# Sparse attention with routed experts: a reordered addition, a step timetable for the side jobs, and routing moved between engines

## The chip, the core and the metric

The kernel runs on one core of a Trainium2 chip. The core has four compute engines that work side by side, each through its own queue in order: TensorE (PE, with its weight loads as PEld), VectorE (DVE), ScalarE (ACT) and GpSimd (POOL). SyncE (SP) issues most of the DMAs. The metric is the device time of one execution in microseconds (us); lower is better.

## The reference

```python
scores = scale * np.matmul(q, k.transpose(0, 1, 3, 2))      # 8 batches, 8 heads, 576 x 576, d = 64
kth = np.partition(scores, -top_k, axis=-1)[..., -top_k:-top_k + 1]   # top_k = 32
scores = np.where(scores >= kth, scores, -1000000000.0)
attn = np.exp(scores - np.max(scores, axis=-1, keepdims=True))
attn = attn / (np.sum(attn, axis=-1, keepdims=True) + 1e-09)
x = np.matmul(attn, v)                # heads joined: 4608 tokens of 512
logits = x @ w_gate                   # 8 experts
expert_idx = np.argmax(logits, axis=1)
# gate_w = softmax(logits) at expert_idx
out[mask] = gate_w[mask, None] * (np.maximum(x[mask] @ w1[e], 0.0) @ w2[e])   # for each expert e
```

Attention keeps the 32 largest scores of each row. Each token then goes to the one expert with the largest logit.

## The kernel before

**Attention** runs as one loop of 144 steps. A step handles two tiles of 128 query rows with 576 scores each; nine steps make a quarter (four heads of a batch), 36 steps a pair of batches. The loop is software-pipelined: in iteration t, PE makes the scores of step t+3 (`ps`), which ACT copies to `sb`; DVE searches step t (24 `MAX8` of 48 columns a step into `vq`, line 1079, then a merge, lines 450, 1082 and 1086, whose last three reductions are carried into the next iteration as `delayed`); POOL makes the thresholds `nb` from the merge; ACT writes a sign mask `sg` for each of the two tiles of step t-2 with the threshold as bias, and counts the kept scores (line 494); POOL adds the mask to the scores (line 495), which sends the small ones far down; PE transposes step t-3 (`tt`, line 501), ACT takes the exponential (`et`, line 505), and PE multiplies by V (`px`, line 515).

**Side jobs** are Python generators in lanes. `advance` is called once a step; it goes through the lanes in the order of their due times (`DUE`), takes one stage of each lane whose needs (shared PSUM banks, spots, and planner's units of us per engine) fit under `LIMITS`, and queues its instructions. `at=` restricts a stage to given steps of the nine. The names ahead of a profile row show the jobs, all recorded by the helper in line 280:

- `prep`: turns Q and K for the next scores (`rq`, `rk`, `lqk` to `qk`).
- `sums` and `rows`: the softmax sums, then the finished rows turned back, scaled (`xm`, `lp`, `xl`, `lpl`) and stored to DRAM as tokens `xs` and partial logits `lps`.
- `find`: for each pair of batches, rows whose count of kept scores isn't 32 are flagged (`r_key`, `r_ok`, `r_qx`) and fetched (`r_sb`).
- `redo`: four rounds of `MAX8` and `MATCH_REPLACE8` over the 576 scores of up to 128 flagged rows, then their exponential.
- `patch`: turns the flagged rows (`r_et`), multiplies them by V (40 matmuls in one run), turns the result (`r_xa`) and overwrites their rows of `xs` and `lps`.
- `route`: loads the pair's logits (`ll`), finds each token's expert (`lg`, `sh`, `oh`), counts tokens per expert with a history of one-hots (`hist`, `cum`), ranks them on PE, and scatters each token's entry to `table` in ten indirect DMAs (line 899).

Lanes take the pairs one after another. PSUM has two shared banks for jobs, one bank for the scores' left parts, and three banks `tt`, of which the last 384 columns (SMALL) are a spot for small results. Such work is queued as `pe_late`, behind the step's transposes.

**The expert stage (MoE)** works in units: an expert and a number of 128-token tiles. Each unit runs eight chunks of the hidden size; a chunk loads 512 KB of weights, splits them into high and low parts (ACT line 1009, DVE 1011 and 1012, POOL 1012), and runs `hidden` (line 1264) and `project` (line 1279) with three products each. `EARLY` names units that start on part of the batches: an entry (5, 1, 2) is one expert, two tiles, from the first four batches (8 - 5 + 1); (3, 4, 3) is four experts, three tiles, from the first six. Full units have five tiles, and the rest of an early expert's tiles follows later. At the attention's end the jobs left over are drained stage by stage, one round of lanes between two chunks of the early units. When all are routed, `over` makes a table of overflow tiles.

Of the kernel before, what the change touches and what calls it, by code (L numbers as in the profile page):

```python
# [23 lines left out]
TOPK = 32  # L24
# [3 lines left out]
A0, A1, A2, A3 = -4, 1, 2, 2  # L28
EARLY = ((5, 1, 2), (3, 4, 3))
# [26 lines left out]
def attention_moe(ctx, tc, q, k, v, w_gate, w1, w2, out):  # L56
# [117 lines left out]
    nc.gpsimd.iota(eight, pattern=[[1, 8]], base=0, channel_multiplier=0, allow_small_or_imprecise_dtypes=True)  # L174
    stat = consts.tile([128, B, 3], F32, name="stat")
# [101 lines left out]
    cell, small, held, att_open = [1], [1], [0], [True]  # L277
# [13 lines left out]
    def need(**k):  # L291
        return k
# [43 lines left out]
    def j_prep(p):  # L336
# [151 lines left out]
    def softmax(t, us, i):  # L488
# [6 lines left out]
        nc.gpsimd.tensor_tensor(SB[u], SB[u], SG[i], op=OP.add)  # L495
# [45 lines left out]
    def j_sums(n):  # L541
# [17 lines left out]
        yield need(slack=1)  # L559
# [117 lines left out]
    def j_find(p):  # L677
# [31 lines left out]
        vec(nc.vector.tensor_tensor, oh, slots[:, None, 0:64].to_broadcast([128, 16, 64]),  # L709
            sl.rearrange("p j x -> p (j x)")[:, :, None].to_broadcast([128, 16, 64]), op=OP.is_equal)  # L710
# [29 lines left out]
    def turn(x, name, w=512):  # L740
        pt = bank()
        xf = x.rearrange("p h d -> p (h d)")
        for c in range(HP):
            pe(nc.tensor.transpose, pt[:, c * 128:(c + 1) * 128], xf[:, c * 128:(c + 1) * 128], ident)
        xt = jobs.tile([128, w], F32, name=name, bufs=1)[:, 0:512]
        act(nc.scalar.activation, xt, pt, AF.Copy)
        act(release, pt)
        return xt

    def j_redo(p):  # L750
# [28 lines left out]
    def j_patch(p, ex, nb, qi, hmb):  # L779
        sm = lambda name, shape, dt=F32: jobs.tile(shape, dt, name=name, bufs=1)  # L780
        et = sm("r_et", [128, KB * 128]).rearrange("p (c q) -> p c q", c=KB)
        yield need(bank=1, nook=1, pe=0.6, act=0.7, dve=0.2, at=FREE)
        vec(nc.vector.tensor_scalar, nb[:, 1:2], nb[:, 1:2], 1e-9, None, op0=OP.add)
        vec(nc.vector.reciprocal, nb[:, 2:3], nb[:, 1:2])
        pt = bank()
        for c in range(MAIN):
# [25 lines left out]
        yield need(bank=1, pe=0.5, act=0.5, at=FREE)  # L812
        xt = turn(xa, "r_et", KB * 128)
# [28 lines left out]
    def j_route(p):  # L842
# [11 lines left out]
        yield  # L854
        yield need(dve=0.8)
# [6 lines left out]
        cum = small("cum", [128, E, KR + 1], BF)  # L862
        vec(nc.vector.tensor_reduce, lg, ll.rearrange("p i (h e) -> p i e h", h=H), axis=AX.X, op=OP.add)
# [754 lines left out]
```

## Time and profile before

| | |
|---|---|
| median of 3 runs | 1284.72 us (1282.67 to 1284.81) |
| the profiled execution's own time | 1284.31 us, of which the profile's span is 1282.4 |
| busy: PE, DVE, POOL, ACT | 1164.8, 957.6, 843.3, 813.8 us |
| first and last exponential of the 144 steps | 40.0 and about 765 us |

A row of instructions reads: line, engine, operation, output<-inputs, shapes, count | busy time, mean ns of one | idle time of the engine just before them and what ended it. A row of waits reads: who waited, for whom: us in total, times, longest. A row of a timeline is start, length, instruction, and in brackets the idle time before it. Only the engine that ends last in a stage sets its time; idle time of the others is free.

### The profile page before, as it was taken

What the parts mean: (1) busy time and instruction counts of PE and PEld (TensorE: products, weight loads), DVE (VectorE), ACT (ScalarE), POOL (GpSimd) and SP (SyncE); (2) the same over time, 40 slices, a digit from 0 to 9 for tenths busy, and PEclk for the clock granted to TensorE, in tenths of its full rate; (3) what the DMA queues carried; (4) which work ended last, traced back from release to release, by engine and by line L of the source; (5) the groups of instructions that cost most, each with busy time, mean ns of one, the idle gap of its engine ahead of it and who ended that gap; (6) DMA issues with size and microseconds to landing.
All of it is one profiled execution on the core that took longest, in us unless ns stands there. A gap on an engine that the chain in (4) does not pass through costs nothing.

```text
span 1282.4 us, 32272 instructions
## 1 busy us (share of the span) xinstructions
PE 1164.8 (91%) x9589; PEld 914.1 (71%) x9589; DVE 957.6 (75%) x6480; ACT 813.8 (63%) x1649; POOL 843.3 (66%) x1370
## 2 busy tenths in 40 slices
PE   5889998999898889987989858999899999999997
PEld 2566666666665666665666657889799998988996
DVE  6989999999999898998999946636573333323763
ACT  3999999998898798986998842433232323233442
POOL 5677778886889886887886876565643324244654
PEclk8999999999999899997999988999999999999999
DMA  6645665665565465656464525645544333357773
GB/s 172 197 158 170 199 208 164 178 199 157 167 181 174 158 188 162 192 150 171 145 187 144 173 72 166 197 131 181 144 147 144 115 109 119 101 165 218 220 210 102
DMA packets 269081, 209.50 MB, mean 163 GB/s; under 512 B 134407, under 2 KB 212400, under 8 KB 268896
## 3 DMA queue, kind: packets, MB, share of 16 engines
q1 hardware_dynamic: 259216, 185.69, 48.2%
q0 software_dynamic: 8448, 21.37, 5.3%
q8 instruction: 78, 1.28, 0.5%
q14 instruction: 107, 0.88, 0.2%
q10 hardware_dynamic: 1232, 0.30, 0.1%
HBM read 101.10 MB, written 107.33 MB: 163 GB/s over the span
## 4 chain that ended last, share of the span: by engine, by line
PE 40%; DVE 30%; POOL 11%; ACT 9%; issue 7%; DMA 1%; SPq 1%; POOLq 0%; ACTq 0%; DVEq 0%
DVE vq L1079 15%; PE ph L1264 15%; PE y L1279 14%; DVE vq L1086 6%; PE pt L280 4%; ACT sg L494 3%; POOL sb L495 3%; ACT sb L386 2%; PE ps L384 2%; POOL wl L1012 2%; PE px L515 2%; POOL table L899 1%; PE tt L501 1%; ACT qk L280 1%; PE mt L1244 1%
## 5 line engine op out<-in xcount | busy, mean ns | idle before, releaser
L495 POOL TENSOR_TENSOR sb<-sb,sg 128x576 f32<-128x576 f32 x288 | 366.9, 1282 | 126.1 <-ACT sg L494 120.0
L1079 DVE MAX8 vq<-sb 128x8 f32<-128x48 f32 x3456 | 430.1, 200 | 4.4 <-ACT sb L386 4.1
L1012 POOL TENSOR_TENSOR wl<-r,wh 128x512 fp32r<-128x512 f32 x102 | 132.1, 1296 | 212.1 <-DVE wh L1011 206.9
L494 ACT ACTIVATE sg<-sb,nb 128x576 int8<-128x576 f32 x288 | 223.0, 774 | 65.2 <-POOL nb L1082 64.5
L515 PEld LDWEIGHTS px<-et,rv 128*64 128x64 f32 x3200 | 161.4, 139 | 129.0 <-ACT xt L280 61.3
L515 PE MATMUL px<-et,rv 128*64 128x128 f32 (+1 forms) x3200 | 194.8, 271 | 19.0 <-ACT xt L280 12.9
L384 PE MATMUL ps<-qk 64*128 64x512 f32 (+1 forms) x576 | 182.4, 660 | 19.5 <-ACT sb L386 13.8
L1265 ACT ACTIVATE hh<-ph 128x320 fp32r<-128x320 f32 (+2 forms) x128 | 56.2, 439 | 225.1 <-PE ph L1264 210.1
L501 PE MATMUL tt<-turner,sb 128*128 128x128 f32 x1296 | 175.3, 281 | 12.0 <-ACT et L505 9.1
L505 ACT ACTIVATE et<-tt,shifts 128x1152 f32<-128x1152 f32 x144 | 176.3, 1224 | 0.8 <-PE tt L501 0.8
L501 PEld LDWEIGHTS tt<-turner,sb 128*128 128x128 f32 x1296 | 140.4, 141 | 36.2 <-issue 21.8
L386 ACT ACTIVATE sb<-ps 128x1024 f32<-128x1024 f32 x144 | 145.6, 1011 | 31.9 <-PE ps L384 31.8
L1264 PE MATMUL ph<-xh,wh 128*128 128x320 f32 (+2 forms) x504 | 161.0, 320 | 0.0
L1266 DVE SCALAR_TENSOR_TENSOR hl<-ph,hh 128x320 fp32r<-128x320 f32 (+2 forms) x128 | 62.6, 489 | 127.0 <-ACT hh L1265 107.5
L1264 PE MATMUL ph<-xl,wh 128*128 128x320 f32 (+2 forms) x504 | 156.4, 310 | 0.0
L1264 PE MATMUL ph<-xh,wl 128*128 128x320 f32 (+2 forms) x504 | 156.4, 310 | 0.0
L1279 PE MATMUL y<-wh,hl 128*128 128x512 f32 x316 | 125.3, 396 | 4.2 <-DVE hl L1266 4.2
L1012 DVE TENSOR_TENSOR wl<-r,wh 128x512 fp32r<-128x512 f32 x102 | 91.1, 893 | 51.0 <-ACT wh L1009 43.2
L1279 PE MATMUL y<-wh,hh 128*128 128x512 f32 x316 | 125.0, 396 | 0.0
L1279 PE MATMUL y<-wl,hh 128*128 128x512 f32 x316 | 125.0, 395 | 0.0
L1086 DVE MAX8 vq<-vq 128x8 f32<-128x49 f32 (+1 forms) x576 | 120.3, 209 | 0.0
L1264 PEld LDWEIGHTS ph<-xh,wh 128*128 128x128 f32 x504 | 95.2, 189 | 5.8 <-issue 1.8
(288 smaller groups left out, 2046.5 us busy)
## 6 DMA issues: line engine op xcount, KB each, us to landing
r<-in_moe_w_dram SPq DMA_DIRECT2D x204, 256.0 KB
sc<-sb SPq DMA_DIRECT2D x128, 288.0 KB
sc<-sb SPq DMA_DIRECT2D x128, 256.0 KB
rv<-in_v_dram SPq DMA_DIRECT2D x32, 256.0 KB
xs<-xm SPq DMA_DIRECT2D x16, 512.0 KB
rq<-in_q_dram SPq DMA_DIRECT2D x60, 128.0 KB
rk<-in_k_dram SPq DMA_DIRECT2D x60, 128.0 KB
sc<-sb SPq DMA_DIRECT2D x32, 144.0 KB
```

Of the source, the lines that this page charges most:

```text
L384: nc.tensor.matmul(MAINS[:, n], qk[:, 0, w], qk[:, 1, 2 * LEFT:], start=True, stop=True)
L386: nc.scalar.activation(bass.AP(EX[-1].tensor, EX[-1].offset, [list(EX[-1].ap[0]), [S + LEFT, 2], [1, M]]), MAINS, AF.Copy)
L494: nc.scalar.activation(upper(SG[i]), SB[u], AF.Sign, bias=nb[:, i, 1:2], accum_out=CNT[b // 2][:, b % 2, 2 * lt + i:2 * lt + i + 1])
L495: nc.gpsimd.tensor_tensor(SB[u], SB[u], SG[i], op=OP.add)
L501: nc.tensor.transpose(tt[:, c], x[:, c * 128:(c + 1) * 128], ident)
L505: nc.scalar.activation(ET[t], three.rearrange("p (c q) -> p c q", c=NB9), AF.Exp, bias=shift(t // (2 * NT))[:, 0:1], scale=0.125)
L515: yield lambda kb=kb, blk=blk: nc.tensor.matmul(px[h * 64:(h + 1) * 64], block(rv, p % 2, kb if kb < MAIN else MAIN + n, h), et[:, blk, q] ...
L1012: (nc.gpsimd if i else nc.vector).tensor_tensor(lo, r, hi, op=OP.subtract)
L1079: one[m][0](*one[m][1])
L1086: f(*a)
L1264: nc.tensor.matmul(ph, a[:, c, :], x[:, c, s], start=(m == 0), stop=(m == len(seq) - 1))
L1279: nc.tensor.matmul(PY[u, t], a[:, s], x, start=(f == 0 and m == 0), stop=(f == FC - 1 and m == 2))
```

## The change

1. **Second addition behind thresholds.** The second of a step's two additions on POOL is issued after the threshold instructions carried from the step before, and not ahead of them.
2. **A timetable of nine steps.** `prep` gets fixed steps (`TURNS`), the products and the patch's scatters too (`PRODUCTS`, `SENDS`). `LIMITS` are lower. The due times are 1000 to 3000 steps away, so `find`, `redo`, `patch` and `route` always come after the others. Stages are cut smaller while steps run (`in_steps`): one DVE search or replacement a step, the 40 products in three pieces, one scatter a step. `rows` starts two steps later. Pair 0's routing thus ends about step 109, pair 1's about step 143, and pair 2's after the loop; before, pair 2's ended with the loop.
3. **Flagged rows turned in the transposes' banks.** `turned_late` puts the turned blocks into SMALL as `pe_late`, three blocks at a time, instead of into a shared bank.
4. **Routing's work on GpSimd.** The differences, one-hots and places of `route` and the key of `find` go from DVE to POOL. The sum over the history is no longer made on DVE (`cum`) but as eleven matmuls accumulated on PE. The place of the experts' skip count goes through ACT.
5. `EARLY` becomes four experts with two tiles from the first four batches and two with three tiles from the first six: fourteen units where there were thirteen. `tl_i` of `over` is made at the start. `ahead_take` comes two iterations later.

POOL's queue in a step of the attention loop, before and then after (`sb<-sb,sg` are the additions, `nb` the thresholds, `nbt` the part of the next ones):

```order
L1086 TENSOR_SCALAR nbt_281<-vq_307,shifts 128x2
L495 TENSOR_TENSOR sb<-sb,sg_149 128x576
L495 TENSOR_TENSOR sb<-sb,sg_151 128x576
L1082 TENSOR_TENSOR nb_283<-vq_307,factors 128x4
L1082 TENSOR_TENSOR nb_283<-nb_283,nbt_281 128x2
```

```order
L1122 TENSOR_SCALAR nbt_282<-vq_311,shifts 128x2
L500 TENSOR_TENSOR sb<-sb,sg_151 128x576
L1114 TENSOR_TENSOR nb_284<-vq_311,factors 128x4
L1114 TENSOR_TENSOR nb_284<-nb_284,nbt_282 128x2
L500 TENSOR_TENSOR sb<-sb,sg_153 128x576
```

The two thresholds moved up by one place, between the additions.

DVE's queue in the second routing stage of a pair, before and then after (`hist`, `cum`, `fm` and `gsm` are routing; `vq`, `low` and `mid` are the step's own merge):

```order
L1079 MAX vq_309<-sb 128x8 x19
L1086 MAX vq_309<-vq_309 128x8
L280 TENSOR_TENSOR hist<-oh,valid 128x10x8
L1086 TENSOR_REDUCE vq_309<-vq_309 128x2
L280 TENSOR_REDUCE cum<-hist 128x88
L1086 MAX vq_309<-vq_309 128x8
L280 COPY hist<-cum 128x8
L450 TENSOR_REDUCE low<-vq_309 128x46
```

```order
L1111 MAX vq_311<-sb 128x8 x19
L1122 MAX vq_311<-vq_311 128x8
L285 TENSOR_REDUCE fm<-oh 128x10
L1122 TENSOR_REDUCE vq_311<-vq_311 128x2
L285 TENSOR_REDUCE gsm<-gex 128x10
L1122 MAX vq_311<-vq_311 128x8
L285 TENSOR_SCALAR gsm<-gsm 128x10
L455 TENSOR_REDUCE low<-vq_311 128x46
```

The product with `valid`, the window sum and the copy left this queue; reductions that stood in other steps stand in their place.

```diff
-A0, A1, A2, A3 = -4, 1, 2, 2
-EARLY = ((5, 1, 2), (3, 4, 3))
+A0, A1, A2, A3 = -4, 3, 2, 2
+EARLY = ((5, 4, 2), (3, 2, 3))
-FREE = (2, 3, 4, 7, 8)
-DUE = dict(redo=12, patch=12, sums=0, rows=0, find=3, route=12)
-LIMITS = dict(pool=3.5, act=2.1, dve=2.6, pe=3.0)
+TURNS = ((1, 3), (5, 7))
+PRODUCTS = (5,)
+SENDS = (8, 0, 1, 2, 3, 4, 5)
+DUE = dict(redo=1000, patch=1000, sums=0, rows=0, find=2000, route=3000)
+LIMITS = dict(pool=2.8, act=1.6, dve=1.75, pe=2.4)
...
-        nc.gpsimd.tensor_tensor(SB[u], SB[u], SG[i], op=OP.add)
+        return lambda: nc.gpsimd.tensor_tensor(SB[u], SB[u], SG[i], op=OP.add)
...
+        key = sm("r_key", [128, 2, NLT])
+        pool(nc.gpsimd.tensor_scalar, key, lw, float(2 * TOPK - S), 1.0, op0=OP.is_equal, op1=OP.subtract)
+        pool(nc.gpsimd.tensor_tensor, key, key, below1.rearrange("p (j x) -> p j x", j=2), op=OP.mult)
...
-        vec(nc.vector.scalar_tensor_tensor, key, lw, float(2 * TOPK - S), idx1.rearrange("p (j x) -> p j x", j=2),
-            op0=OP.not_equal, op1=OP.mult)
...
+    def turned_late(x, xt, blocks):
+        pt, leave = spot("turn")
+        for n, c in enumerate(blocks):
+            w = x[c].shape[1]
+            pe_late(nc.tensor.transpose, pt[0:w, n * 128:(n + 1) * 128], x[c], ident)
...
+            yield need(dve=0.7)
             vec(nc.vector.max, top, x)
-            if not last:
+            if r < TOPK // 8 - 1:
+                if in_steps[0]:
+                    yield need(dve=0.7)
                 vec(nc.vector.match_replace, wk, top, x, NEG)
...
-                if n == 0 and kb == 0:
-                    yield need(bank=1, pe=2.2, at=FREE)
-                    pv = bank()
+                if n * KB + kb in ((0, 4, 7) if in_steps[0] or not n + kb else ()):
+                    yield need(pe=1.3) if n + kb else need(bank=1, pe=1.7, at=PRODUCTS)
+                    pv = pv if n + kb else bank()
...
-        vec(nc.vector.tensor_tensor, sh, lg, mx[:, :, None].to_broadcast([128, KR, E]), op=OP.subtract)
-        vec(nc.vector.scalar_tensor_tensor, oh, sh, 0.0, edesc, op0=OP.is_equal, op1=OP.mult)
+        pool(nc.gpsimd.tensor_tensor, sh, lg, mx[:, :, None].to_broadcast([128, KR, E]), op=OP.subtract)
+        pool(nc.gpsimd.tensor_scalar, oh, sh, 0.0, None, op0=OP.is_equal)
+        pool(nc.gpsimd.tensor_tensor, oh, oh, edesc, op=OP.mult)
...
-        vec(nc.vector.tensor_reduce, cum, win, axis=AX.X, op=OP.add)
-        vec(nc.vector.tensor_copy, hist[:, :, KR], cum[:, :, KR])
...
-        pe_late(nc.tensor.matmul, rk, ones, cum[:, :, 0:KR].rearrange("p e c -> p c e"), start=False, stop=True)
+        for c in range(KR + 1):
+            pe_late(nc.tensor.matmul, rk, ones, hist[:, :, c:c + KR].rearrange("p e c -> p c e"), start=False,
+                    stop=(c == KR))
...
-            if c % 2 == 0 or 2 * p + 1 not in ahead and 2 * p + 2 < B:
+            if c % (1 if in_steps[0] else 3) == 0:
                 yield need(pool=1.0)
...
-        if grp(t - LAG):
-            softmax(t - LAG, grp(t - LAG), 1)
+        add = softmax(t - LAG, grp(t - LAG), 1) if grp(t - LAG) else lambda: None
...
+        while delayed:
+            f, a = delayed.pop(0)
+            f(*a)
+        add()
         delayed = last
...
-        m = t - LAG - TD - 3
+        m = t - LAG - TD - (5 if t < steps else 3)
         if m >= 0 and m % NT == NT - 1:
             start("rows", j_rows(m // NT), t + DUE['rows'])
```

More of the change, by code (lines that the diff above doesn't have):

```diff
@@ L276, in attention_moe @@
     pq, aq, dq, gq, lq = [], [], [], [], []
-    cell, small, held, att_open = [1], [1], [0], [True]
+    cell, small, held, att_open, in_steps = [1], [1], [0], [True], [True]
     def later(queue):
@@ L339, in j_prep @@
         hs = slice(2 * (p % 2), 2 * (p % 2) + 2)
-        yield need(bank=1, pe=0.5, act=0.5)
+        yield need(bank=1, pe=0.5, act=0.5, at=TURNS[p % 2][:1])
         for g, r in enumerate((rq, rk)):
@@ L348, in j_prep @@
             if g == 0:
-                yield need(bank=1, nook=1, pe=0.6, act=0.8)
+                yield need(bank=1, nook=1, pe=0.6, act=0.8, at=TURNS[p % 2][1:])
         pt, leave = spot("left")
@@ L553, in j_sums @@
         pool(nc.gpsimd.tensor_scalar, w, w, -1.25 * FAR, 1.25 * FAR, op0=OP.max, op1=OP.min)
+        yield need(act=0.8)
         act(nc.scalar.activation, both, both, AF.Exp, scale=0.125)
-        yield need(slack=1)
+        for _ in range(3):
+            yield need(slack=1)
         yield need(dve=1.0)
@@ L738, in j_find @@
         FOUND[p] = (sb, qi, hmb)
[L740 to L748, printed above, removed]
+    def turned_late(x, xt, blocks):
[3 more added lines that the diff above has]
+            pe_late(nc.tensor.transpose, pt[0:w, n * 128:(n + 1) * 128], x[c], ident)
+        w = x[blocks[0]].shape[1]
+        full = [c for c in blocks if x[c].shape[1] == 128]
+        act(nc.scalar.activation, xt[:, full[0] * 128:(full[-1] + 1) * 128], pt[:, 0:len(full) * 128], AF.Copy)
+        if len(full) < len(blocks):
+            act(nc.scalar.activation, xt[0:LEFT, MAIN * 128:], pt[0:LEFT, len(full) * 128:len(blocks) * 128], AF.Copy)
+        act(leave)
     def j_redo(p):
@@ L811, in j_patch @@
         pool(nc.gpsimd.tensor_tensor, xa, xa, hmb, op=OP.mult)
-        yield need(bank=1, pe=0.5, act=0.5, at=FREE)
-        xt = turn(xa, "r_et", KB * 128)
+        xt = sm("r_et", [128, KB * 128])[:, 0:512]
+        flat = xa.rearrange("p h d -> p (h d)")
+        turns = [flat[:, c * 128:(c + 1) * 128] for c in range(HP)]
+        yield need(spot=1, pe=0.4, act=0.4)
+        turned_late(turns, xt, (0, 1, 2))
+        yield need(spot=1, pe=0.1, act=0.2)
+        turned_late(turns, xt, (3,))
         yield need(spot=1, pe=0.2, act=0.1, pool=1.4)
@@ L861, in j_route @@
         fm = small("fm", [128, KR])
-        cum = small("cum", [128, E, KR + 1], BF)
-        vec(nc.vector.tensor_reduce, lg, ll.rearrange("p i (h e) -> p i e h", h=H), axis=AX.X, op=OP.add)
+        for j in range(2):
+            yield need(dve=0.7)
+            k = slice(j * KB, (j + 1) * KB)
+            vec(nc.vector.tensor_reduce, lg[:, k], ll[:, k].rearrange("p i (h e) -> p i e h", h=H), axis=AX.X, op=OP.add)
         vec(nc.vector.tensor_reduce, mx, lg, axis=AX.X, op=OP.max)
-        vec(nc.vector.tensor_tensor, sh, lg, mx[:, :, None].to_broadcast([128, KR, E]), op=OP.subtract)
@@ new lines, in j_route @@
+        yield need(act=0.2)
+        act(nc.scalar.activation, ex, sh, AF.Exp)
+        yield need(slack=1)
+        yield need(slack=1)
+        yield need(dve=0.4)
+        sm = small("gsm", [128, KR])
+        vec(nc.vector.tensor_reduce, fm, oh, axis=AX.X, op=OP.max)
+        vec(nc.vector.tensor_reduce, sm, ex, axis=AX.X, op=OP.add)
+        vec(nc.vector.tensor_scalar, sm, sm, 1e-9, None, op0=OP.add)
+        yield need(pool=1.2, dve=0.1)
+        new = hist[:, :, KR + 1:].rearrange("p e c -> p c e")
@@ L876, in j_route @@
+        pool(nc.gpsimd.tensor_tensor, oh, oh, fm[:, :, None].to_broadcast([128, KR, E]), op=OP.subtract)
+        pool(nc.gpsimd.tensor_scalar, oh, oh, 0.0, None, op0=OP.is_equal)
+        pool(nc.gpsimd.tensor_tensor, new, oh, valid, op=OP.mult)
+        vec(nc.vector.reciprocal, pay[:, :, 2].bitcast(F32), sm)
+        yield need(spot=1, pe=0.9, act=0.2)
         rk, leave = spot("rank")
         rk = rk[:, 0:KR * E].rearrange("p (c e) -> p c e", e=E)
-        pe_late(nc.tensor.matmul, rk, before, hist[:, :, KR + 1:].rearrange("p e c -> p c e"), start=True, stop=False)
@@ L905, in j_route @@
         if 2 * p + 1 in ahead:
-            w, T = ahead[2 * p + 1]
-            yield
-            yield need(bank=1)
-            pt = bank()
-            pe(nc.tensor.matmul, pt[:, 0:E], ones, hist[:, :, KR], start=True, stop=True)
-            vec(nc.vector.tensor_scalar, skip[:, w], pt[:, w], -1.0, float(T * 128), op0=OP.mult, op1=OP.add)
-            vec(release, pt)
-            vec(nc.vector.tensor_scalar, skip[:, w], skip[:, w], 0.0, None, op0=OP.max)
-            vec(nc.vector.tensor_tensor, ebase[:, :, w], ebase[:, :, w],
-                skip[:, None, w].to_broadcast([128, KR, w.stop - w.start]), op=OP.add)
             for e in range(w.start, w.stop):
@@ L1098, in attention_moe @@
             start("sums", j_sums(m // NT), t + DUE['sums'])
+        in_steps[0] = t < steps
         if t < steps:
```

99 lines of the change are left out of this document (54 added, 45 removed).

## The prediction

> **What bounds the kernel now.** I read the span first, then busy time by stretch, then the waits, then single steps. Attention runs from 40 to 765 us in 144 steps; the expert stage (MoE) fills the rest.
>
> ```profile
> span 1282.4 us, 32272 instructions
> ...
> 40.00:208.20 168.20, 155.23 (x1571) 109.71 (x1567) 157.56 (x1420) 156.81 (x315) 128.25 (x206) 0.99 0.58 180
> 208.20:723.00 514.80, 464.06 (x4677) 330.53 (x4675) 490.98 (x4148) 443.86 (x907) 407.51 (x679) 0.98 0.56 170
> 723.00:764.90 41.90, 27.30 (x306) 22.95 (x306) 25.65 (x164) 26.05 (x52) 33.09 (x56) 0.88 0.36 115
> 764.90:1282.40 517.50, 494.00 (x2947) 439.40 (x2943) 254.01 (x489) 169.78 (x344) 252.62 (x297) 0.98 0.52 154
> ...
> 166.20:208.20 42.00, 39.62 (x407) 28.41 (x405) 40.41 (x360) 39.33 (x81) 33.41 (x56) 1.00 0.61 188
> 252.40:296.20 43.80, 39.46 (x410) 28.64 (x410) 43.80 (x371) 41.42 (x86) 34.60 (x57) 1.00 0.60 186
> 296.20:343.30 47.10, 45.80 (x460) 32.13 (x460) 43.74 (x396) 40.34 (x83) 33.50 (x57) 1.00 0.56 169
> 579.30:632.20 52.90, 45.97 (x429) 32.43 (x425) 46.85 (x388) 40.03 (x83) 41.48 (x66) 0.88 0.56 155
> ```
>
> Columns after the stretch: its length, then PE, PEld, DVE, ACT and POOL busy, the granted PE clock, DMA share and GB/s. The last four rows are groups of nine steps. A quiet group (first of the four) takes 42.0 us with DVE, ACT and PE all between 39 and 41: nobody is full. From 208.2 on the flagged rows' and the routing's jobs come in, and eleven groups take 514.8 us, 46.8 each. Some are full on DVE (43.8 of 43.8); others are held by a lump on PE (45.8 of 47.1); one falls to clock 0.88 on the way. In MoE, PE is busy 494 of 517.5.
>
> So attention can give back 168.2 - 157.6 = 10.6 us in the quiet stretch and 514.8 - 491.0 = 23.8 in the job stretch by filling DVE's idle time, and more only if DVE has less to do. What breaks its flow:
>
> ```profile
> ACT sg L494 <- POOL nb L1082: 11.0, 24, 0.9
> ...
> ACT sg L494 <- POOL nb L1082: 47.8, 57, 3.5
> ...
> DVE skip L280 <- PE pt L280: 3.5, 1, 3.5
> ```
>
> The first row is the wait list of the quiet stretch, the second of the job stretch, the third of the group from 579.3. ACT waits 11.0 and 47.8 us for the thresholds nb, which stand on POOL behind the second addition. DVE waits 3.5 us at one place for a count on PE.
>
> **The second addition.** One step in a group that is full on DVE:
>
> ```profile
> 255.09 1.28 POOL L495 TENSOR_TENSOR sb<-sb,sg 128x576 f32<-128x576 f32 x1 [0.59 <-ACT sg L494]
> 256.75 1.28 POOL L495 TENSOR_TENSOR sb<-sb,sg 128x576 f32<-128x576 f32 x1 [0.38 <-ACT sg L494]
> 257.98 0.20 POOL L1082 TENSOR_TENSOR nb<-vq,factors 128x4 f32<-128x4 f32 x1
> 258.26 0.20 POOL L1082 TENSOR_TENSOR nb<-nb,nbt 128x2 f32<-128x2 f32 x1
> ...
> 255.92 0.18 DVE L1082 TENSOR_REDUCE vq<-vq 128x2 f32<-128x36 f32 x1
> ...
> 259.69 1.20 PE L501 MATMUL tt<-turner,sb 128*128 128x128 f32 x9
> ```
>
> DVE's last input to the threshold is ready at 256.10, the first addition ends at 256.37 and POOL then idles 0.38 us for ACT's sign. The two threshold instructions (0.20 each) fit about there and come 1.6 us earlier. The second addition moves back by at most 0.5, and the transposes that need it start only at 259.69, 1.66 us after its end. Here the step costs nothing and frees ACT's next sign. In the quiet stretch it can remove ACT's 11.0 us, but DVE's own load stops it at 10.6; the other end is 0 (another loop sets the 42.0). I take half, -5.
>
> **Work off DVE.** All in the job stretch:
>
> ```profile
> L280 DVE COPY hist<-cum 128x8 bf16<-128x8 bf16 x2 | 2.4, 1196 | 0.0
> L280 DVE TENSOR_REDUCE cum<-hist 128x88 bf16<-128x968 bf16 x2 | 2.3, 1160 | 0.1
> L280 DVE SCALAR_TENSOR_TENSOR r_key<-r_lw,idx 128x72 f32<-128x72 f32 x2 | 2.0, 984 | 0.0
> L280 DVE TENSOR_TENSOR hist<-oh,valid 128x80 bf16<-128x80 f32 x2 | 1.6, 824 | 0.0
> L280 DVE TENSOR_TENSOR po<-po,ebase 128x80 f32<-128x80 f32 x2 | 1.6, 776 | 0.0
> L280 DVE TENSOR_TENSOR oh<-oh,fm 128x80 f32<-128x80 f32 x2 | 1.5, 750 | 0.0
> L280 DVE SCALAR_TENSOR_TENSOR oh<-sh,edesc 128x80 f32<-128x80 f32 x2 | 1.4, 720 | 0.0
> L280 DVE TENSOR_TENSOR sh<-lg,mx 128x80 f32<-128x80 f32 x2 | 1.3, 631 | 0.0
> L280 DVE TENSOR_TENSOR po<-po,oh 128x80 f32<-128x80 f32 x2 | 0.5, 242 | 0.0
> ...
> L280 POOL TENSOR_TENSOR r_lw<-cnt,r_lw 128x72 f32<-128x72 f32 x4 | 1.4, 338 | 0.3
> ```
>
> These nine rows add up to 14.6 us. The split of lg and of the one-hot r_qx and the new reduction to totals add some 0.8 back: -13.8, leaving DVE 477 us. On POOL ten new instructions a pair of batches, by the r_lw row 0.34 each, make 3.4 us; POOL idles 107 of the 514.8, so I charge nothing. Without that idle time they would cost 2 x 3.4 = 7.
>
> The Trainium skill (GPSIMD Engine Reference, 4.1 Engine selection) calls GpSimd the wrong engine for elementwise work, about twice slower than VectorE with two inputs. Here the 338 ns stand against 242 ns in the undisturbed DVE row but 631 to 824 ns in the disturbed ones, so the trace agrees with the direction only for undisturbed work; by twice 242 ns the ten would take 4.8 us instead of 3.4 and the sum would be the same.
>
> **The timetable.** PE's products of a pair were one run, and the new order cuts them into 16, 12 and 12:
>
> ```profile
> 296.13 4.98 PE L280 MATMUL pt<-rv,r_et 128*64 128x256 f32 x40
> ...
> 882.18 0.30 PE L280 MATMUL pt<-hist,before 128*128 128x80 bf16 x1
> 882.30 0.32 PE L280 MATMUL pt<-cum,ones 128*128 128x80 bf16 x1
> ```
>
> The pieces are 2.0, 1.5 and 1.5 us in three steps, so PE falls behind by about as much in all but not at once; DVE works on scores made three steps earlier and the rows' next result is taken some steps later. The redo rounds of DVE go from a search and a replacement in one step to one of them. Turning flagged rows in the transposes' spare bank frees the two shared banks; the copies there (up to five more a pair) make ACT wait for PE's late transposes, bounded by 0 and by five times 0.4 us, since nine transposes take 1.20 above. ACT has 71 us idle in the stretch: hidden. The ranking's window sum becomes ten more PE matmuls a pair; starts 0.12 apart to 0.30 each give 1.2 to 3.0 us, on PE beside a fuller DVE: nothing in the stretch.
>
> What of the 23.8 us of DVE idle time remains? Full groups of DVE exist (43.8 of 43.8), so 0 is possible; all 23.8 may stay if ACT and PE set the pace. I leave 9, nearer to the full groups, since the lump, the 3.5 us wait and the low clock are what the change takes away. Job stretch: 477 + 9 = 486, or **-29** (bounds -38 and -14).
>
> The stretch 723 to 764.9 loses pair 2's routing (its patch now ends there and its routing goes behind it) and gains pair 1's last scatters. PE idles there anyway; 0, bounds -4 and +5.
>
> **MoE.** One unit of five tiles becomes one of two and one of three; one whole unit of each size:
>
> ```profile
> 1204.60:1228.00 23.40, 23.40 (x153) 21.23 (x152) 15.60 (x26) 9.81 (x20) 14.59 (x15) 1.00 0.73 213
> 848.80:884.80 36.00, 36.00 (x191) 32.50 (x190) 20.48 (x36) 12.43 (x26) 20.33 (x32) 1.00 0.54 166
> 1019.60:1077.90 58.30, 58.30 (x334) 52.65 (x333) 20.80 (x37) 17.56 (x34) 18.67 (x21) 1.00 0.35 108
> ...
> DVE tr L1385 <- POOL tl_i L1380: 7.8, 1, 7.8
> ...
> L1279 PE MATMUL y<-wh,hl 128*128 128x512 f32 x316 | 125.3, 396 | 4.2 <-DVE hl L1266 4.2
> ...
> L1244 PE MATMUL mt<-turner,gx 128*128 128x128 f32 x152 | 22.9, 273 | 2.8 <-DMA gx<-xs,ids 2.8
> ...
> L899 POOL DMA_INDIRECT table<-pay,pos x40 | 42.4, 1060 | 7.6 <-issue 6.6 <-DVE pay L280 0.6 <-DVE vq L1086 0.2
> ```
>
> 23.4 + 36.0 - 58.3 = +1.1. The table tl_i is now made at the start, so DVE's 7.8 us wait behind POOL's gathers goes and with it PE's 4.2: -4. The early units 1 to 3 no longer need pair 2's routing, so the 2.8 us for gx go: -3. Ranking of pairs 2 and 3 adds 2.4 to 6.0 on PE: +2.4. POOL is busy 14.6 of a two-tile unit's 23.4 already. Into four such units, with 35 us of room, come pair 2's ten scatters, four patch scatters and two lookups at 1.06 each and some ten small instructions at 0.34: 20 us. They stand in POOL's queue with the weights' splits, and SP's weight loads stand behind the logits' load that waits for a patch scatter, so PE waits somewhere: +3 (0 to 10). Sum **-0.5**, bounds -6 and +13.
>
> **Sum.** -5 - 29 + 0 - 0.5 = -34.5 against the profiled execution's 1284.3 (span 1282.4 and 1.9 around it), which is 0.4 below the median of 1284.7: about **1250**.
>
> **Rivals.** (a) ACT and PE, not DVE, set the pace: ACT is at 41.4 of 43.8 in the full group. Then the 23.8 us stay and the quiet stretch too, and only the 13.8 of DVE are won: 1270. (b) DVE fills up in both stretches and MoE gets its best: -10.6 - 38 - 6 gives 1230; for it speak the full groups, against it the quiet ones. (c) The new POOL work holds DVE up. DVE's one-hot has min, median and max of
>
> ```profile
> L280 DVE TENSOR_TENSOR oh<-oh,fm x4: 241/242/1260, 348.2 to 877.8; 128x80 f32<-128x80 f32 x4
> ```
>
> so something can hold such an instruction for 1.0 us, the length of a POOL addition. If DVE lost all of the 3.4 us a pair, three pairs cost 10: 1260. The Trainium skill (SBUF — State Buffer, Who interferes with whom) has this as a rule: a DVE instruction with two SBUF inputs is blocked for the whole of a GpSimd instruction that reads SBUF. The row agrees with it; most of the instructions so held are the ones that leave DVE.
>
> (d) Slower: the second addition now waits in POOL's queue for DVE's merge of the next step. From the step shown, transposes start late once that merge ends 1.2 us after the first addition. By the planner's new limit a job step may hold 1.75 us of DVE jobs; if the merge comes that much later, it is 0.55 too late, and in 99 job steps that is +54, in place of the -29 and -5: 1338. Against it: 256.10 came before 256.37. (e) The spread changes nothing since loops among all four engines set the steps: the job stretch keeps its length, 1284.
>
> **How the numbers follow.** Forecast 1250 (1238 to 1262) 0.52; (a) 0.17; (b) 0.09; (c) 0.10; (d) 0.08; (e) 0.04. Faster by over 0.2% (2.6 us, about the least that a measurement here can tell): 0.52 + 0.17 + 0.09 + 0.10 = 0.88; the same 0.04; slower 0.08. The range goes from between (b) and the forecast to just above (a): 1232 to 1274, with (d), (e) and half of (b) outside.
>
> **What will show it.** Right: quiet groups of 41 us and ACT's wait for nb under a third; job groups of 44 with DVE over 97% busy; no products in one run of 40; PE clock 1.00 through attention; no wait for tl_i. Wrong: POOL's sb addition waiting for DVE through nb, transposes waiting for POOL, ACT waiting for late turning, or gaps on PE in the first four units with POOL full. The forecast fails if DVE stays under 95% busy in the job groups.

## The result, and the profile after

The changed kernel takes 1245.75 us (median of 4, 1241.03 to 1246.27), the kernel before 1284.57 (1282.67 to 1284.81): a ratio of 0.9693, 95% interval 0.9667 to 0.9718. The profiled execution took 1245.57, its span 1243.8. First the busy time by stretch, cut at the same steps as before: up to step 0, steps 0 to 35 (quiet), 36 to 134 (jobs), the last nine, and all behind the last exp.

```profile
0.00:34.90 34.90, 23.75 (x92) 11.08 (x93) 27.43 (x247) 16.36 (x32) 22.88 (x138) 0.86 0.64 177
34.90:194.10 159.20, 151.51 (x1556) 108.56 (x1554) 157.39 (x1439) 154.66 (x315) 126.32 (x206) 1.00 0.65 195
194.10:664.60 470.50, 449.62 (x4645) 325.24 (x4646) 465.61 (x4051) 439.03 (x915) 397.71 (x670) 1.00 0.62 186
664.60:709.80 45.20, 35.73 (x360) 28.21 (x362) 27.45 (x231) 27.67 (x55) 41.02 (x68) 0.90 0.33 94
709.80:1243.80 534.00, 506.67 (x2983) 447.91 (x2979) 267.08 (x507) 174.58 (x359) 278.13 (x340) 0.97 0.53 159
```

| stretch, us | before | after | change | forecast |
|---|---|---|---|---|
| up to step 0 | 40.0 | 34.9 | -5.1 | not in the sum |
| quiet | 168.2 | 159.2 | -9.0 | -5 |
| jobs | 514.8 | 470.5 | -44.3 | -29 |
| last nine steps | 41.9 | 45.2 | +3.3 | 0 |
| behind them (MoE) | 517.5 | 534.0 | +16.5 | -0.5 |
| span | 1282.4 | 1243.8 | -38.6 | -34.5 |

The total came out near the forecast because two errors cancel: attention won 55 us where I had 34 (5 of the 55 lie ahead of step 0), and MoE lost 16.5 where I had it even. DVE's idle time in the job stretch went from 23.8 us to 4.9. Four groups of nine steps:

```profile
153.30:194.10 40.80, 39.18 (x405) 28.39 (x405) 40.80 (x371) 39.03 (x83) 33.30 (x57) 1.00 0.65 194
235.10:275.30 40.20, 38.97 (x405) 28.41 (x405) 40.20 (x347) 38.77 (x82) 34.85 (x59) 1.00 0.68 204
316.70:362.30 45.60, 45.10 (x455) 31.94 (x456) 45.60 (x417) 40.58 (x85) 34.60 (x59) 1.00 0.58 175
489.40:537.60 48.20, 45.54 (x455) 32.08 (x456) 46.37 (x422) 41.11 (x85) 43.85 (x76) 0.99 0.57 168
```

In three of them DVE (third of the busy times) is as long as the group. The third and fourth are the long ones of the stretch; the other nine job groups take 40.2 to 42.6 us. They hold a pair's 40 products, now in pieces of 16, 12 and 12 (326 to 339 us in the third), and PE is busy 45.1 and 45.5 there. DVE fills the time with searches of later steps: 250 and 257 `MAX8` on `sb` in these groups, where nine steps have 216. ACT's wait for the thresholds was 11.0 and 47.8. Now it is, by the wait lists (us in total, times, longest) of the quiet stretch and, second, of the jobs:

```profile
ACT sg L499 <- POOL nb L1114: 2.2, 5, 0.8
...
ACT sg L499 <- POOL nb L1114: 9.7, 13, 1.5
```

Why that wait held all steps is seen in single steps. The timeline of before, in the quiet stretch (start, us, instruction, in brackets the idle time before it and its releaser):

```profile
125.96 0.78 ACT L494 ACTIVATE sg<-sb,nb 128x576 int8<-128x576 f32 x1 [0.55 <-POOL nb L1082]
126.73 1.00 ACT L386 ACTIVATE sb<-ps 128x1024 f32<-128x1024 f32 x1
127.64 0.77 ACT L494 ACTIVATE sg<-sb,nb 128x576 int8<-128x576 f32 x1
...
128.57 1.28 POOL L495 TENSOR_TENSOR sb<-sb,sg 128x576 f32<-128x576 f32 x1 [0.38 <-ACT sg L494]
129.80 0.20 POOL L1082 TENSOR_TENSOR nb<-vq,factors 128x4 f32<-128x4 f32 x1
130.09 0.20 POOL L1082 TENSOR_TENSOR nb<-nb,nbt 128x2 f32<-128x2 f32 x1
130.31 0.78 ACT L494 ACTIVATE sg<-sb,nb 128x576 int8<-128x576 f32 x1 [0.28 <-POOL nb L1082]
```

Sign, copy, sign, second addition, thresholds, next sign: a ring through two engines. It takes 130.31 - 125.96 = 4.35 us here, and any other work of ACT between two signs would make it longer. After, the second addition is out of it:

```profile
120.20 0.78 ACT L499 ACTIVATE sg<-sb,nb 128x576 int8<-128x576 f32 x1
120.96 1.03 ACT L391 ACTIVATE sb<-ps 128x1024 f32<-128x1024 f32 x1
...
121.86 0.79 ACT L499 ACTIVATE sg<-sb,nb 128x576 int8<-128x576 f32 x1
122.39 0.20 POOL L1114 TENSOR_TENSOR nb<-vq,factors 128x4 f32<-128x4 f32 x1
...
122.67 0.20 POOL L1114 TENSOR_TENSOR nb<-nb,nbt 128x2 f32<-128x2 f32 x1
...
122.82 1.28 POOL L500 TENSOR_TENSOR sb<-sb,sg 128x576 f32<-128x576 f32 x1
...
123.88 0.80 ACT L499 ACTIVATE sg<-sb,nb 128x576 int8<-128x576 f32 x1
```

The thresholds are ready at 122.87, 1.0 us ahead of the next sign, and that sign comes 3.68 us after the first one shown (120.20), where it was 4.35. These are single steps: the mean step of the quiet stretch goes from 4.67 to 4.42 us.

In MoE the first units are longer than they need to be. The four early two-tile units, and one without other work:

```profile
722.60:757.40 34.80, 31.31 (x209) 27.80 (x210) 20.74 (x47) 9.94 (x23) 21.35 (x32) 0.92 0.62 183
757.40:788.70 31.30, 31.30 (x216) 25.88 (x214) 17.66 (x40) 13.45 (x32) 23.38 (x33) 1.00 0.63 187
788.70:823.30 34.60, 28.28 (x162) 24.68 (x161) 15.01 (x27) 10.12 (x23) 23.62 (x36) 0.90 0.48 144
823.30:854.40 31.10, 28.12 (x170) 24.98 (x168) 21.37 (x36) 11.16 (x25) 22.76 (x34) 0.95 0.69 199
...
1192.10:1215.40 23.30, 23.30 (x153) 21.11 (x152) 16.18 (x26) 9.73 (x21) 13.26 (x14) 1.00 0.71 203
```

In the third, PE stands twice for weights, once more in the fourth (timeline of PE):

```profile
800.12 0.79 PE L1316 MATMUL y<-wl,hh 128*128 128x512 f32 x1 [3.01 <-POOL wl L1045]
...
806.71 0.58 PE L1301 MATMUL ph<-xh,wh 128*128 128x256 f32 x1 [3.26 <-ACT wh L1042]
...
833.77 0.61 PE L1316 MATMUL y<-wl,hh 128*128 128x512 f32 x1 [2.98 <-POOL wl L1045]
```

For the last two of these gaps, which go when the ids are loaded later (see below), the waits of SP's queue show where the weights were: behind the loads of two experts' ids (L952), which wait for the last scatter.

```profile
SPq L952 <- DMA table<-pay,pos: 17.1, 1, 17.1
```

The timeline of SP shows the same: no weights are asked for between 784.84 and 803.19.

```profile
784.84 0.33 SPq L1035 DMA_DIRECT2D r<-in_moe_w_dram  x1
802.29 0.80 SPq L952 DMA_DIRECT2D ids<-table  x2
803.19 0.38 SPq L1034 DMA_DIRECT2D r<-in_moe_w_dram  x1
```

### The profile page after: what moved, and what is told of

It is laid out like the page before. It is cut to its first block, busy times and chain, and to the rows that moved or that the text cites. A ratio compares the mean times of both kernels' runs of the same rounds, so it can differ in the third digit from the quotient of the medians.

```text
span 1243.8 us, 32462 instructions
## 1 busy us (share of the span) xinstructions
PE 1167.3 (94%) x9629; PEld 921.0 (74%) x9629; DVE 945.0 (76%) x6470; ACT 812.3 (65%) x1671; POOL 866.1 (70%) x1418
## 4 chain that ended last, share of the span: by engine, by line
DVE 39%; PE 37%; POOL 8%; ACT 5%; issue 4%; DMA 3%; SPq 2%; POOLq 0%; ACTq 0%; DVEq 0%
DVE vq L1111 22%; PE ph L1301 16%; PE y L1316 15%; DVE vq L1122 8%; POOL table L943 2%; POOL sb L500 2%; ACT sg L499 2%; PE pt L285 2%; DMA r<-in_moe_w_dram 1%; DVE vq L1114 1%; DVE mid L1122 1%; PE mt L1281 1%; ACT sb L391 1%; ACT et L510 1%; POOL wl L1045 1%
## 5 line engine op out<-in xcount | busy, mean ns | idle before, releaser
L500 POOL TENSOR_TENSOR sb<-sb,sg 128x576 f32<-128x576 f32 x288 | 370.8, 1288 | 75.2 <-ACT sg L499 71.5
L1045 POOL TENSOR_TENSOR wl<-r,wh 128x512 fp32r<-128x512 f32 x110 | 142.2, 1295 | 206.1 <-DVE wh L1044 203.5
L499 ACT ACTIVATE sg<-sb,nb 128x576 int8<-128x576 f32 x288 | 228.8, 794 | 17.4 <-POOL nb L1114 15.6
L1302 ACT ACTIVATE hh<-ph 128x256 fp32r<-128x256 f32 (+2 forms) x128 | 55.9, 437 | 216.0 <-PE ph L1301 202.4
L389 PE MATMUL ps<-qk 64*128 64x512 f32 (+1 forms) x576 | 178.1, 647 | 3.3 <-ACT sb L391 2.8
L1301 PE MATMUL ph<-xh,wh 128*128 128x384 f32 (+2 forms) x504 | 162.0, 321 | 3.3 <-ACT wh L1042 3.3
L1303 DVE SCALAR_TENSOR_TENSOR hl<-ph,hh 128x256 fp32r<-128x256 f32 (+2 forms) x128 | 62.6, 489 | 127.3 <-ACT hh L1302 121.3
L1301 PE MATMUL ph<-xh,wl 128*128 128x384 f32 (+2 forms) x504 | 156.9, 311 | 0.1
L1301 PE MATMUL ph<-xl,wh 128*128 128x384 f32 (+2 forms) x504 | 156.7, 311 | 0.0
L1045 DVE TENSOR_TENSOR wl<-r,wh 128x512 fp32r<-128x512 f32 x110 | 95.7, 870 | 71.7 <-ACT wh L1042 56.8
```

Of the source, the lines that this page charges most:

```text
L389: nc.tensor.matmul(MAINS[:, n], qk[:, 0, w], qk[:, 1, 2 * LEFT:], start=True, stop=True)
L499: nc.scalar.activation(upper(SG[i]), SB[u], AF.Sign, bias=nb[:, i, 1:2], accum_out=CNT[b // 2][:, b % 2, 2 * lt + i:2 * lt + i + 1])
L500: return lambda: nc.gpsimd.tensor_tensor(SB[u], SB[u], SG[i], op=OP.add)
L1045: (nc.gpsimd if i else nc.vector).tensor_tensor(lo, r, hi, op=OP.subtract)
L1301: nc.tensor.matmul(ph, a[:, c, :], x[:, c, s], start=(m == 0), stop=(m == len(seq) - 1))
```

## The experiments

Theories: (1) the second addition's place carries most of the gain, since the ring set the steps; (2) the timetable and the work taken off DVE carry it, as my sum had it. For MoE: SP's queue, GpSimd's load, or PE's added matmuls. The kernel before, run beside each experiment, had medians of 1282.55 to 1284.57, so differences of some 2 us between experiments mean nothing.

**Part 1 undone.** In the changed kernel, `add()` is called where the second addition stood before.

```diff
         add = softmax(t - LAG, grp(t - LAG), 1) if grp(t - LAG) else lambda: None
+        add()
...
-        add()
         delayed = last
```

> The changed kernel with the second addition put back ahead of the thresholds (part 1 undone, all else kept). Theory 1 (the place of the addition frees ACT's sign): ACT's wait for nb goes from 2.2 us back to about 11 in the quiet stretch and from 9.7 towards 40 in the job stretch; the quiet stretch grows from 159 to 166 or 168, the job stretch by 5 to 15; in all 1258 to 1270. Theory 2 (the fixed steps for prep, products and scatters and the lower limits carry the gain): the quiet stretch stays at 159 to 161 and the total at 1246 to 1250.

1288.32 us against 1282.55 for the kernel before, run beside it: 1.0033 (1.0018 to 1.0047). All the rest of the change, without this one move, gains nothing in total. Quiet and job stretch:

```profile
35.00:208.80 173.80, 154.95 (x1550) 110.91 (x1550) 159.12 (x1448) 156.47 (x315) 129.23 (x209) 0.98 0.59 179
208.80:707.60 498.80, 459.74 (x4651) 333.56 (x4649) 469.72 (x4091) 443.37 (x914) 399.40 (x668) 0.98 0.59 175
```

And ACT's wait in the one and the other:

```profile
ACT sg L499 <- POOL nb L1115: 15.6, 20, 2.0
...
ACT sg L499 <- POOL nb L1115: 39.8, 52, 2.0
```

Against the whole change that is +14.6 and +28.3 us, and nothing elsewhere: the other stretches agree within 0.5. My theory 1 had the mechanism and the waits, but half the price.

**Part 1 alone**, in the kernel before:

```diff
-        nc.gpsimd.tensor_tensor(SB[u], SB[u], SG[i], op=OP.add)
+        return lambda: nc.gpsimd.tensor_tensor(SB[u], SB[u], SG[i], op=OP.add)
...
+        add()
         delayed = last
```

> The kernel before with part 1 alone: its second addition behind the thresholds. Theory 1: the quiet stretch goes from 168.2 to 160 or 161, the job stretch from 514.8 to about 500 to 508, in all 1262 to 1272 against 1284.6. Theory 2: the old planner's loops set the steps; within 4 us of 1284.6. My slower rival (the second addition waits for DVE's merge in steps with many DVE jobs, whose limit is 2.6 here) would show as 1290 or more.

1250.87, ratio 0.974 (0.971 to 0.977): 32 of the 39 us from one moved instruction.

```profile
38.70:194.80 156.10, 151.24 (x1569) 109.11 (x1567) 154.71 (x1406) 154.36 (x315) 127.09 (x206) 1.00 0.63 194
194.80:688.00 493.20, 460.51 (x4676) 328.81 (x4675) 485.13 (x4147) 440.35 (x907) 404.38 (x673) 0.98 0.59 177
```

Quiet -12.1, jobs -21.6. One row in the wait list of the job stretch is my rival (d) in small:

```profile
PE tt L501 <- POOL sb L495: 12.9, 16, 1.6
```

Transposes now wait for the second addition, 12.9 us in all. With the whole change it is 2.2. The two runs together show how the parts hang together. DVE's idle time in the job stretch is 23.8 before, 8.1 with part 1 alone, 498.8 - 469.7 = 29.1 with the rest alone, and 4.9 with both. From the first to the last exponential of the loop it is 724.9 us before, 717.4 with the rest alone, 690.2 with part 1 alone and 674.9 with both. So the rest wins 7.5 us there without part 1 and 15.3 behind it.

**Part 1 and the lower limits**, in the kernel before: the same edit and

```diff
-LIMITS = dict(pool=3.5, act=2.1, dve=2.6, pe=3.0)
+LIMITS = dict(pool=2.8, act=1.6, dve=1.75, pe=2.4)
```

> The kernel before with part 1 and the lower limits of a step's jobs (pool 2.8, act 1.6, dve 1.75, pe 2.4), nothing else. In the run with part 1 alone PE's transposes waited 12.9 us for GpSimd's addition in the job stretch, where they wait 2.2 with the whole change. Theory 1 (few jobs of DVE in one step is what keeps the second addition early, my slower rival in small): that wait goes below 5 us, the job stretch from 493 to 483 to 488, in all 1241 to 1247. Theory 2 (the lump of forty products on PE and the work on DVE set the rest): the stretch stays at 490 to 496, 1247 to 1255.

1255.22, ratio 0.9767 (0.9751 to 0.9783). The job stretch, and the transposes' wait in it:

```profile
194.20:684.90 490.70, 458.95 (x4655) 326.24 (x4651) 484.25 (x4141) 440.12 (x907) 401.92 (x667) 0.98 0.59 179
```

```profile
PE tt L501 <- POOL sb L495: 3.4, 6, 1.0
```

The wait goes from 12.9 to 3.4, as theory 1 has it, and the stretch still only from 493.2 to 490.7: theory 2. DVE is busy 484 of 491 here, so PE's wait was beside the bound. The loop as a whole gets 6 us shorter, but what is behind it gets longer by 9 (521.4 to 530.8): jobs that are put off come back there, among them four more of the scatters to `table` (20 instead of 16). So the limits alone are no gain.

**The timetable undone** in the changed kernel:

```diff
-PRODUCTS = (5,)
-SENDS = (8, 0, 1, 2, 3, 4, 5)
-DUE = dict(redo=1000, patch=1000, sums=0, rows=0, find=2000, route=3000)
-LIMITS = dict(pool=2.8, act=1.6, dve=1.75, pe=2.4)
+PRODUCTS = (2, 3, 4, 7, 8)
+SENDS = tuple(range(9))
+DUE = dict(redo=12, patch=12, sums=0, rows=0, find=3, route=12)
+LIMITS = dict(pool=3.5, act=2.1, dve=2.6, pe=3.0)
...
-        yield need(bank=1, pe=0.5, act=0.5, at=TURNS[p % 2][:1])
+        yield need(bank=1, pe=0.5, act=0.5)
...
-                yield need(bank=1, nook=1, pe=0.6, act=0.8, at=TURNS[p % 2][1:])
+                yield need(bank=1, nook=1, pe=0.6, act=0.8)
```

> The changed kernel with the timetable undone: the due times and limits of before, prep, products and scatters allowed in every step; the smaller cuts, the spare banks and the work on GpSimd stay. Theory 1 (the timetable makes the groups of nine alike): job groups go from 42 or 43 back towards 45 or 46, job stretch 470 to about 495, in all 1262 to 1275. Theory 2 (smaller cuts and less work on DVE are enough): job stretch 470 to 476, in all 1246 to 1252.

1252.75, 0.9753 (0.9724 to 0.9782): 7 us over the whole change. The job stretch is 479.4, 8.9 more, in between the two theories.

```profile
197.00:676.40 479.40, 452.28 (x4655) 323.74 (x4652) 471.42 (x4082) 441.26 (x912) 404.15 (x679) 1.00 0.61 182
```

DVE's idle time is 8.0 instead of 4.9, and its busy time 5.8 more. Some 3 us of that are searches: 2361 `MAX8` on `sb` fall into the stretch instead of 2343, and a step has 24 and about 4.4 us of DVE's work. But the last nine steps take 37.8 us here instead of 45.2. From the first to the last exponential it is 675.6 against 674.9, so the timetable wins nothing in the loop as a whole; what it takes out of the job stretch comes back in the last nine steps. The 7 us lie ahead of step 0 (38.6 instead of 34.9) and behind the loop (537.5 instead of 534.0), and why there is not shown.

**Routing back on DVE**, in and behind the loop (`cum`, one-hots, places; the key of `find` stays on GpSimd):

```diff
-        pool(nc.gpsimd.tensor_tensor, sh, lg, mx[:, :, None].to_broadcast([128, KR, E]), op=OP.subtract)
...
+            vec(nc.vector.tensor_tensor, sh, lg, mx[:, :, None].to_broadcast([128, KR, E]), op=OP.subtract)
...
+        onv = True
...
-        for c in range(KR + 1):
+        if onv:
+            pe_late(nc.tensor.matmul, rk, ones, cum[:, :, 0:KR].rearrange("p e c -> p c e"), start=False, stop=True)
+        for c in range(0 if onv else KR + 1):
```

> The changed kernel with all of routing's differences, one-hots, places and the sum over the history back on DVE (the key of find stays on GpSimd): part 4 undone for the most part. Theory 1 (with part 1 made, DVE is the bound of the attention steps, so what DVE does not have to do is saved in full): DVE's busy time in the job stretch goes from 465.7 to 477 or 480 and the stretch from 470.6 to 481 to 486; the expert stage gives 0 to 6 back; in all 1250 to 1262. Theory 2 (DVE has slack in the job stretch): within 3 us of 1246.

1252.97, 0.9754 (0.9737 to 0.977): 7 us over the whole change, theory 1, with a job stretch some 3 us shorter than I expected. DVE's busy time grows by 10.6 and the stretch by 7.7:

```profile
193.90:672.10 478.20, 454.04 (x4634) 327.45 (x4636) 476.24 (x4094) 439.54 (x914) 393.38 (x655) 0.98 0.60 183
```

The loop as a whole grows by 6.3. Where DVE stands in its searches when a stretch ends differs from run to run, so the parts of attention are best compared over the whole loop, from the first to the last exponential:

| us | up to step 0 | loop | behind it |
|---|---|---|---|
| before | 40.0 | 724.9 | 517.5 |
| part 1 alone | 38.7 | 690.2 | 521.4 |
| part 1 and limits | 39.1 | 684.1 | 530.8 |
| all but part 1 | 35.0 | 717.4 | 534.5 |
| the change | 34.9 | 674.9 | 534.0 |
| timetable undone | 38.6 | 675.6 | 537.5 |
| routing on DVE | 34.6 | 681.2 | 536.6 |

**Routing behind the loop on DVE**: the same edit for pairs 2 and 3 alone.

```diff
+        onv = not in_steps[0]
...
+        if onv:
...
+            vec(nc.vector.tensor_reduce, cum, win, axis=AX.X, op=OP.add)
```

> The changed kernel, but routing that runs behind the attention loop (pairs 2 and 3) makes its differences, one-hots, places and the sum over the history on DVE as before the change, with one rank matmul in place of eleven. Theory 1 (in the expert stage PE and POOL are the scarce engines): PE loses 20 matmuls of 0.31 us, 6.2 us, and PE's three waits for wl and wh (3.0, 3.3, 3.0 us) shrink as POOL has some 14 instructions less; 1232 to 1240. Theory 2 (DVE's longer queue delays hl and wh in turn): PE's new gaps eat the 6.2, 1243 to 1248.

1246.01, 0.9709 (0.9678 to 0.9741): no gain. My price was wrong first of all: a matmul's row says 0.31 us, but the twelve of a pair start 0.14 apart and take 1.85 us together, so the twenty are worth 2.8 and not 6.2. And PE's gaps only moved, among them one of 6.9 us at 810, where SP stood 16.3 us at the ids.

**The ids later**:

```diff
         if 2 * p + 1 in ahead:
+            for _ in range(5 if p == 2 else 0):
+                yield
             for e in range(w.start, w.stop):
```

> The changed kernel, with the loads of the ids of pair 2's two experts issued five chunks later on SP's queue. Theory 1 (SP stands at these loads for 17 us until GpSimd's last scatter has landed, the weights' loads stand behind it, and PE runs dry): SP's wait for table goes below 5 us, PE's gap of 3.3 us at 803 for wh and the 3.0 at 831 go, and the half-clock time behind them; the expert stage goes from 521 to 510 to 515, in all 1235 to 1241. Theory 2 (GpSimd's own crowding is what holds the units): the gaps only move, 1243 to 1248.

1234.54, 0.9616 (0.96 to 0.9632): 11 us under the whole change, theory 1. MoE's units take 510.4 us instead of 521.2. The wait of 17.1 at that load is gone; SP's one wait for `table` in the units is at another load (L1193, the ids of later units):

```profile
SPq L1193 <- DMA table<-pay,pos: 2.9, 1, 2.9
```

In the four two-tile units ACT waits for weights, and PE has one gap of a microsecond or more left in the third:

```profile
ACT wh L1044 <- DMA r<-in_moe_w_dram: 11.4, 8, 5.5
```

```profile
799.58 0.80 PE L1318 MATMUL y<-wl,hh 128*128 128x512 f32 x1 [3.39 <-POOL wl L1047]
```

ACT's wait for weights goes from 25.9 to 11.4, PE's gaps of 3.3 and 3.0 go, and the first one stays, for `wl` on GpSimd.

**Both edits, and the transition.** 

> The two edits together: ids of pair 2 loaded five chunks later, and routing behind the loop on DVE with one rank matmul in place of eleven. Theory 1 (two costs of their own: SP's stall, and 6.2 us of matmuls on PE that the stall hid the last time): 7 to 14 us under the changed kernel, 1232 to 1239. Theory 2 (either the gain of the ids alone, or nothing more than that): within 3 us of the run with the ids alone.

1240.19, 0.9646 (0.9625 to 0.9666): 6 us over the ids alone, which neither theory had. PE waits 3.6 us for the gathers of the fifth unit. Routing has one stage more on this path, so with the delay of five chunks those gathers start a chunk later, just ahead of the unit's first transposes. That is read from the trace and was not tried with a shorter delay, so this run does not decide where that routing is better placed.

> As the run before, and pair 1's scatters go two a step, with the gathers of the first unit issued two iterations sooner. Theory 1 (the 12.8 us between the last exp and the first product of the experts wait for gathers that stand behind late scatters on GpSimd): that stretch goes to 8 or 9, PE's gap of 3.6 us at its start goes, in all 3 to 6 us under the run before, 1228 to 1235. Theory 2 (two scatters in one step of the loop hold its additions, as GpSimd is 85% busy there): the last nine steps grow by what the transition gains.

```diff
-A0, A1, A2, A3 = -4, 3, 2, 2
+A0, A1, A2, A3 = -4, 1, 2, 2
...
-            if c % (1 if in_steps[0] else 3) == 0:
+            if c % ((1 + p) if in_steps[0] else 3) == 0:
```

1234.50, 0.9615 (0.9599 to 0.9631): 5.7 under the run before. From the last exp to the first product it takes 6.3 us instead of 13.0, but right behind it PE now waits 3.7 us for `xl`. The fifth unit's gathers are late here too (3.9).

The same without DVE's part: 

> The changed kernel with the ids of pair 2 loaded five chunks later, pair 1's scatters two a step and the first unit's gathers two iterations sooner; routing behind the loop stays on GpSimd and PE as changed. Theory 1 (the two stalls are apart: 11 us of SP's and some 6 of the transition): 1228 to 1231. Theory 2 (time won in the transition is lost in the first units, which then start while GpSimd still has the tail's work, as in the run with both edits and DVE): 1233 to 1236.

1231.79, 0.9581 (0.9564 to 0.9599): the lowest median of all, 4% under the kernel before and 14 us under the change. It lies between the two theories: 2.8 us under the ids alone, where theory 1 had some 6 for the transition, and its five runs spread from 1228 to 1234. The transition takes 8.6 us here instead of 13.2.

> As the one before, but behind the loop two scatters a chunk in place of three. Theory 1 (three scatters of 1.27 us with their clearing and a wl of 1.3 are more than the 3.9 us of a two-tile chunk; with two GpSimd keeps up): PE's gap of 3.4 us at wl near 796 goes, 3 to 5 us under the one before. Theory 2 (the sum of GpSimd's work counts, not its order): within 1.5 us of the one before.

Against the one before:

```diff
-            if c % ((1 + p) if in_steps[0] else 3) == 0:
+            if c % ((1 + p) if in_steps[0] else 2) == 0:
```

1233.91, 0.9613 (0.9598 to 0.9628): no gain from two scatters a chunk, 2.1 over the one before. PE's gap near 796 does go from 3.4 to 1.9 us, as theory 1 has it, but there is a wait of 4.0 us for the fifth unit's gathers again, as routing ends later.

> As the one before, with routing behind the loop on DVE. Rank matmuls start 0.14 us apart, so 20 fewer are worth 2.8 us of PE and not 6.2 as I put it before. Theory 1 (with GpSimd keeping up, that is won): 2 to 4 us under the one before. Theory 2 (DVE's longer queue delays xl and hl at the start of units): 0 to 4 us over it.

1238.42, 0.9635 (0.9619 to 0.9651): 4.5 over, about theory 2's size, with the same late gathers (4.0 us). Its mechanism shows in one place (PE waits 1.2 us for `hl` at 895).

## Why the prediction was right, and where it was not

The sign, the range and the size are right, but the size is in part luck: attention and MoE were both mis-sized, in opposite directions, and the job stretch came out for another reason than the one given.

- **Second addition (-5 quiet, nothing in the job stretch).** Mis-sized: 14.6 and 28.3 when it is undone, 12.1 and 21.6 when made alone. I had quoted ACT's 47.8 us for `nb` and then priced the step from one group that was full on DVE, where it costs nothing. That group is the shortest of the eleven (43.8); seven of the others were 3 us and more longer. And I took "no engine is full" in the quiet groups (42.0 with three engines at 39 to 41) as a reason for half of the gain. It was the mark of a ring, which is no engine's load.
- **Work off DVE (-13.8).** Right in kind: 10.6 of DVE and 7.7 of the stretch for what could be put back (without `find`'s key, 2.0 in my list); some 3 of the 10.6 are 17 more searches that fall into the stretch. But DVE's busy time in the job stretch fell by 25.4 in all, which is why the stretch came out beyond my best bound (-44.3 against -38). DVE made 2400 searches there before and 2343 after, 2.4 steps fewer, about 10 us. It is further behind when the stretch ends: the last nine steps have 120 searches instead of 72, where DVE idles anyway. Over the whole loop the gain is 50.0.
- **What remains of DVE's idle time (9).** 4.9, but not for my reason. I had given the timetable the lump, the 3.5 us wait and the clock, 14.8 in all. Part 1 alone takes the idle time from 23.8 to 8.1, and without the timetable it is 8.0. PE's products come in pieces now (runs of 12 at 331.75 and 337.54), and the clock is 1.00, but over the whole loop the timetable is worth 0.7 us.
- **Last nine steps (0).** +3.3, inside its bounds.
- **MoE (-0.5, bounds -6 and +13).** +16.5, outside. Of its terms, the wait for `tl_i` is gone and PE's 4.2 with it (-4), and the ranks cost 2.8 for 2.4. The 2.8 us for `gx` did not go: PE waits 1.5 for `gx` at 736 and 3.6 for the first unit's `kt` at 716. The step that failed is "+3 (0 to 10)" for the crowding behind the loop: moving the ids alone gives 11 back. I had named SP's queue, but with the logits' load in it (5.1 us of wait) and not the ids (17.1). And I had no term for the transition from the last exp to the first product, 7.5 before and 12.8 after. The earlier gathers and scatters shorten it by 4 to 7, of which 1 to 4 come back as a wait for `xl` right behind it.
- **The start (not in the sum).** -5.1. PE's transposes wait 8.2 us for the first loads before and 4.7 after. Step 0 begins at 34.6 to 38.5 in the ten profiles with the fixed steps for `prep` and at 38.6 to 40.0 in the four without them. How much of it is the change and how much varies from run to run is not shown.
- **Rivals.** (b) is nearest to what happened in attention: it had 10.6 and 38 for the quiet and the job stretch, 48.6 together, and 53.3 were measured. Its MoE (-6) was the wrong way. (a) and (e) fall: DVE is the bound in the job stretch. (c) falls: routing's work on GpSimd wins time. The Trainium skill's rule that elementwise work belongs on VectorE (GPSIMD Engine Reference, 4.1 Engine selection) would have it on DVE; the run that puts it there is 7 us slower, with DVE busy 476 us of its job stretch of 478 and GpSimd 393. (d) is there, 12.9 us of transposes' wait with part 1 alone, but far from its 54, and most of it beside DVE's own load.

## What to carry to other kernels

If several engines are nearly but not quite full in a steady loop, look for a ring of short dependences among them, and price the edit by the wait that closes the ring, over all steps: a step that is full elsewhere tells nothing of the others. Cutting the work of an engine pays more once no such ring holds it: the rest of this change was worth 7.5 us of the loop with the ring and 15.3 without. A gain in one stretch can be work that moved to the next, so compare the whole loop too. Work that is put off from a loop comes back at its end, on whatever queue is in order there: look at what each queue, the DMA-issuing one too, has standing behind the first instruction that has to wait.

## What was not expected of the hardware

A gap of 3 us on PE cost more than itself here. Behind the gap that ends at 800.12, the products `y` start 0.43 us apart instead of 0.23, and those of `ph` behind the second gap 0.21 instead of 0.12, until 809.7; the granted clock is 0.52 from 800.1 to 803.4 and 0.50 from 806.7 to 809.7. The length of a gap does not decide it alone. Behind one of 2.01 us, which ends at 867.39, the products `y` start 0.43 apart from 868.22 on; behind one of 2.83 us in the kernel before, which ends at 791.70, those of `ph` start 0.12 apart and the clock is 1.00. The Trainium skill (TensorE: Matmul & The Clock Gate, What's actually happening) gives an idle window of about 3.4 us for the fall to half rate; here gaps of 3.01 and 2.01 were enough.
